# Attention operands of an eight-head kernel: the high half of v written by VectorE from the loaded v, and q and k copied by one ScalarE instruction

## The chip, the core and the metric

The kernel runs on one core of a Trainium2 chip. A core has five engines that run their own instruction queues in order and wait for each other by semaphores: PE (TensorE: matmuls and transposes into PSUM), DVE (VectorE), ACT (ScalarE), POOL (GpSimd) and SP, which here only issues transfers. Sixteen DMA engines move data between memory and the core, and also transpose blocks of 16-bit values. The metric is the time of one execution on the device in microseconds (us); lower is better.

## What is computed

An attention layer with a bias that a small network makes from positions, then two feed-forward blocks (a Fourier mixing block and a gated block), each on 4 batches of 576 positions. The change touches the attention alone:

```python
B, H, S, D = 4, 8, 576, 64
scores = (1 / np.sqrt(D)) * np.matmul(q, k.transpose(0, 1, 3, 2))
scores = scores + bias                      # one 576x576 bias per head, from w1, b1, w2
scores = scores - np.max(scores, axis=-1, keepdims=True)
attn = np.exp(scores)
attn = attn / (np.sum(attn, axis=-1, keepdims=True) + 1e-09)
attn_out = np.matmul(attn, v)
# ... attn_out then goes through two feed-forward blocks on 512 columns
```

## The kernel before

**Numbers in two halves.** Single-precision products are made from parts that TensorE multiplies fast. A value is split into a high half (the value rounded to a shorter form) and a low half (the value minus its high half), and a product is the sum of three matmuls: high by high, high by low, low by high. For q and k the short form is fp32r, for v and for the exponentials it is fp16. v is first multiplied by a power of two, `vs`, that `v_scale` finds from all of v.

**Stages.** The bias phase comes first (`bias_phase`, 48 blocks): POOL, ACT and PE make masks and products, and DVE evicts each block of bias into memory on the core (`evict`). Attention follows, in 72 steps `d` of two units each. A unit is one tile of 128 positions of one head. Sixteen pairs of heads (4 batches by 4 pairs) pass through the steps, two pairs in nine steps; step `c = d % 9` counts within these nine.

**One step of the loop** (the last loop of `attention_phase`; the program order of every engine is the order in which the Python code issues, since the schedule is manual):

- DVE subtracts for the transposed exponentials of the step before (`flip_low`, L477).
- ACT makes the two exponentials `P` of unit pair `d-1` (`soft`, L428).
- PE makes the 12 score matmuls of pair `d` (`scores`, L392), then five transposes `turn` of one unit (`flip`, L468), which ACT rounds to fp16 (`pt`, L470), and the products with v of pair `d-6` (`back`, L494, 28 to 60 small matmuls into `po`).
- For every second pair the transposition goes by DMA: ACT rounds the exponentials (`high`, L439), POOL subtracts the low half (`low`, L445, `hl`), and SP issues a DMA transpose (`turn` in the code, L458).
- DVE adds the bias to the scores and takes the maximum (`total`, L405, `s`), twice.
- At `c` of 3, 4 and 8 of the products (six steps later, so in steps 0, 1 and 5), DVE normalises `po` (`finish`: L514 `ri`, L518, L523 or L532).

The score tiles and the `turn` tile share three PSUM buffers, so that each `turn` waits until `flip_low` has read the one before.

**The preparation of a pair of heads** (`prep`, a generator that the loop advances twice a step, from `c` of 0 and of 5 on): q, k and v of the pair lie in `raw`, loaded by SP steps earlier (`load`). The first advance issues the rounding of k and q on ACT (L366, L367) and the second POOL's low half `kl` (L369). In the next step the third advance, between DVE's two `total`, issues POOL's `ql` (L371), and the fourth, after the second `total` and after `finish` has issued `ri`, issues POOL's scaling of v in place (L374). The fifth advance, a step later, issues ACT's high half of v (L376) and POOL's low half (L377). The first pair's preparation is spread over the bias phase, at blocks 8, 12, 16, 44 and 45.

`P` has four buffers, `hl` three, the halves of q and k two, `vp` (the two halves of v) three.

Of the kernel before, what the change touches and what calls it, by code (L numbers as in the profile page):

```python
# [9 lines left out]
F32 = mybir.dt.float32  # L10
F32R = mybir.dt.float32r
# [3 lines left out]
AF = mybir.ActivationFunctionType  # L15
ALU = mybir.AluOpType
PSUM = bass.MemoryType.PSUM

B, H, S, D = 4, 8, 576, 64
# [33 lines left out]
QW = S + 64  # L53
RAW = 2 * (S + 2 * QW)
# [8 lines left out]
def pool(tc, **kw):  # L63

    return tc.tile_pool(reuse_waits="tile", **kw)
# [263 lines left out]
def attention_phase(tc, nc, io, vs, bias, biasl, raw, xd, ident, after, es, right):  # L329
# [6 lines left out]
    tp = e1.enter_context(pool(tc, name="qk", bufs=2, side="right"))  # L336
    rq, st, live, pts, outs, xs, hls, mms, Ps = {}, {}, {}, {}, {}, {}, {}, {}, {}
# [12 lines left out]
    def load(n, nm):  # L350
        b, p = pairs[n]
        o, w = {"q": (0, QW), "k": (QW, S), "v": (QW + S, QW)}[nm]
        o += RAW // 2 * (n % 2)
        t = raw[:, o : o + w]
        if nm == "v":
            t = t.rearrange("p (t d) -> p t d", t=5)
        nc.sync.dma_start(out=t, in_=io[nm][b, p])
        rq.setdefault(n, {})[nm] = t

    def prep(n):  # L360

        r = rq.pop(n)
        T = {nm: tp.tile([128, S if nm[0] == "k" else QW], F32R, tag=nm, name=nm) for nm in ("kh", "kl", "qh", "ql")}
        T["v"] = vps[n % 3]
        st[n] = T
        nc.scalar.activation(out=T["kh"], in_=r["k"], func=AF.Copy)  # L366
        nc.scalar.activation(out=T["qh"], in_=r["q"], func=AF.Copy)  # L367
        yield
        nc.gpsimd.tensor_tensor(out=T["kl"], in0=r["k"], in1=T["kh"].bitcast(F32), op=ALU.subtract)  # L369
        yield  # L370
        nc.gpsimd.tensor_tensor(out=T["ql"], in0=r["q"], in1=T["qh"].bitcast(F32), op=ALU.subtract)  # L371
        yield
        vv = r["v"].rearrange("p t (h d) -> p t h d", h=2)
        nc.gpsimd.tensor_scalar(out=vv, in0=vv, scalar1=vs[:, 0:1], scalar2=None, op0=ALU.mult)  # L374
        yield
        nc.scalar.activation(out=T["v"][:, :, :, 0:64], in_=vv, func=AF.Copy)  # L376
        nc.gpsimd.tensor_tensor(out=T["v"][:, :, :, 65:129], in0=vv, in1=T["v"][:, :, :, 0:64], op=ALU.subtract)  # L377
        yield

    def scores(d):  # L380
# [155 lines left out]
    def store(d):  # L536
# [8 lines left out]
        for a in range(2):  # L545
            f = 128 * p + (64 * a if ahead(n) else 64 - 64 * a)
            nc.sync.dma_start(out=xd[b][512:S, f : f + 64], in_=x[64 * a : 64 * a + 64, 4, 0:64])

    yield [lambda n=n, nm=nm: load(n, nm) for n in range(2) for nm in "kqv"]
    yield from prep(0)  # L550
    yield True
    wp = es.enter_context(pool(tc, name="att", bufs=3))
# [12 lines left out]
    for d in range(nd + L5 + 2):  # L565
# [8 lines left out]
        n = 2 * (d // 9) + (c >= 5)  # L574
        if us and c in (0, 5) and n + 1 < len(pairs):
            nxt = prep(n + 1)
# [32 lines left out]
        if us and n + 2 < len(pairs):  # L609
            for nm in {0: "k", 1: "q", 2: "v"}.get(c - 5 * (c >= 5), ""):  # L610
                load(n + 2, nm)
# [1298 lines left out]
```

## Time and profile before

| | |
|---|---|
| time, median of 3 runs | 1056.87 us (1053.0 to 1058.15) |
| the profiled execution: its time, its span | 1050.65 us, 1048.9 us |
| mean granted TensorE clock of the profiled execution | 0.987 |
| busy over the span: PE, DVE, ACT, POOL | 94%, 63%, 51%, 29% |
| instructions: PE, DVE, ACT, POOL | 10571, 1736, 1000, 226 |

How to read it: the busy shares are averages over stages that differ. POOL works almost only in the bias phase and in attention, the first third of the span; after that PE is busy nearly without a pause in the feed-forward blocks. The profiled execution was 1.7 us longer than its span, which is what lies around the span.

### The profile page before, as it was taken

The page shows a single profiled execution, that of the slowest core. Times are in us where ns is not written, and L with a number is a line of the kernel's source. Part 1 is how long each engine was busy: PE and PEld are TensorE (multiplying, and loading weights), DVE is VectorE, ACT ScalarE, POOL GpSimd, SP SyncE. Part 2 cuts the span into 40 slices and gives each one's busy share as a digit, 9 for nine tenths or more (in the row PEclk, how much of TensorE's full clock was granted, in tenths as well). Part 3 has the DMA queues.
Part 4 walks back from the last instruction along what each step waited for, and adds up shares of the span by engine and source line. Part 5 has one row for each costly group of instructions (what it writes and reads, how often), then busy time and mean ns, then how long its engine had stood idle before and what let it go on. Part 6 is the DMA issues. An engine that isn't in the chain of part 4 may idle for free.

```text
span 1048.9 us, 25378 instructions
## 1 busy us (share of the span) xinstructions
PE 989.2 (94%) x10571; PEld 910.7 (87%) x10571; DVE 659.7 (63%) x1736; ACT 534.1 (51%) x1000; POOL 303.1 (29%) x226
## 2 busy tenths in 40 slices
PE   9898888988888899899999999999999999999998
PEld 6777787877778677899999999999999898989897
DVE  6888787888788887778944333244962556261611
ACT  6987888989898456444411112122542353334322
POOL 6998777788785000000000000000011111010100
PEclk9999799999999999999999999999999999999999
DMA  9882377889786601335300000001340000001001
GB/s 311 307 292 85 83 173 168 194 187 198 166 184 135 189 23 41 101 122 181 122 1 2 1 1 1 1 2 61 102 137 2 1 1 11 32 11 41 9 33 50
DMA packets 121339, 98.55 MB, mean 94 GB/s; under 512 B 86532, under 2 KB 97032, under 8 KB 121224
## 3 DMA queue, kind: packets, MB, share of 16 engines
q1 hardware_dynamic: 118488, 90.73, 32.3%
q10 hardware_dynamic: 2592, 5.31, 1.4%
q8 instruction: 82, 1.34, 0.5%
q0 software_dynamic: 144, 0.89, 0.2%
q14 instruction: 33, 0.27, 0.1%
HBM read 67.42 MB, written 9.44 MB: 73 GB/s over the span
## 4 chain that ended last, share of the span: by engine, by line
PE 71%; DVE 9%; POOL 7%; ACT 4%; issue 4%; DMA 3%; SPq 1%; ACTq 0%; POOLq 0%; DVEq 0%
PE h L1336 18%; PE acc L1372 18%; PE psp L1508 5%; PE pu L1483 4%; PE po L1530 4%; PE pv L1431 4%; POOL hl L445 3%; PE y L854 3%; PE sc L392 2%; PE bps L272 2%; PE po L494 2%; PE pre L253 2%; DVE pt L477 2%; PE turn L468 2%; PE D L884 2%
## 5 line engine op out<-in xcount | busy, mean ns | idle before, releaser
L1340 ACT ACTIVATE gh<-h 128x256 fp32r<-128x256 f32 x144 | 55.2, 383 | 245.8 <-PE h L1336 240.2
L1341 DVE SCALAR_TENSOR_TENSOR gl<-h,gh 128x256 fp32r<-128x256 f32 x144 | 60.9, 423 | 170.6 <-ACT gh L1340 170.0
L1336 PE MATMUL h<-uh,wh 128*128 128x256 f32 x576 | 161.5, 281 | 2.2 <-DVE gl L1341 2.0
L1372 PE MATMUL acc<-gh,wh 128*128 128x256 f32 x576 | 163.0, 283 | 0.0
L1372 PE MATMUL acc<-gh,wl 128*128 128x256 f32 x576 | 161.0, 280 | 1.4 <-DVE wl L1044 1.4
L1336 PE MATMUL h<-uh,wl 128*128 128x256 f32 x576 | 160.9, 279 | 1.1 <-DVE wl L1044 1.1
L1372 PE MATMUL acc<-gl,wh 128*128 128x256 f32 x576 | 160.8, 279 | 0.0
L1336 PE MATMUL h<-ul,wh 128*128 128x256 f32 x576 | 160.7, 279 | 0.0
L1128 POOL MEMSET w<- 64x288 f32 x2 | 0.7, 335 | 434.5 <-DVE wsq L1025 434.4
L1336 PEld LDWEIGHTS h<-uh,wh 128*128 128x128 f32 x576 | 109.0, 189 | 2.9 <-DVE gl L1341 2.4
L1372 PEld LDWEIGHTS acc<-gh,wl 128*128 128x128 f32 x576 | 108.4, 188 | 1.7 <-DVE wl L1044 1.7
L1336 PEld LDWEIGHTS h<-uh,wl 128*128 128x128 f32 x576 | 108.4, 188 | 1.3 <-DVE wl L1044 1.3
L1372 PEld LDWEIGHTS acc<-gh,wh 128*128 128x128 f32 x576 | 108.9, 189 | 0.4
L1372 PEld LDWEIGHTS acc<-gl,wh 128*128 128x128 f32 x576 | 108.9, 189 | 0.3
L1336 PEld LDWEIGHTS h<-ul,wh 128*128 128x128 f32 x576 | 108.8, 189 | 0.0
L428 ACT ACTIVATE P<-s,mm 128x576 f32<-128x576 f32 x144 | 103.4, 766 | 5.5 <-DVE mm L420 5.3
L445 POOL TENSOR_TENSOR hl<-P,hl 128x1024 f16<-128x1024 f32 x68 | 86.1, 1288 | 19.6 <-ACT hl L439 11.8
L468 PE MATMUL turn<-ident,P 128*128 128x128 f32 x380 | 58.3, 285 | 29.8 <-DVE pt L477 29.4
L494 PE MATMUL po<-vp,pt 128*128 128x65 f16 (+3 forms) x2324 | 83.5, 195 | 2.2 <-DMA pt<-hl 0.8
L494 PEld LDWEIGHTS <-pt 128*128 128x128 f16 (+1 forms) x2324 | 80.1, 101 | 5.6 <-issue 2.0
L243 POOL TENSOR_SCALAR mask<-tx,w,nb 128x576 f16<-128x576 f32 x36 | 81.9, 2286 | 9.8 <-DVE xt L218 6.1
L468 PEld LDWEIGHTS turn<-ident,P 128*128 128x128 f32 x380 | 41.3, 142 | 42.2 <-DVE pt L477 16.1
(252 smaller groups left out, 2507.1 us busy)
## 6 DMA issues: line engine op xcount, KB each, us to landing
w<-in_w_ch SPq DMA_DIRECT2D x32, 512.0 KB, 3.6
tx<-in_c_xm SPq DMA_DIRECT2D x36, 288.0 KB, 5.8
vld<-in_v ACTq DMA_DIRECT2D x16, 320.0 KB, 4.6
raw<-in_q SPq DMA_DIRECT2D x16, 320.0 KB, 4.1
raw<-in_v SPq DMA_DIRECT2D x16, 320.0 KB, 4.4
raw<-in_k SPq DMA_DIRECT2D x16, 288.0 KB, 3.4
xd<-x SPq DMA_DIRECT2D x16, 256.0 KB, 4.1
w<-in_w_in SPq DMA_DIRECT2D x8, 512.0 KB, 3.5
```

The source lines that it names most:

```text
L243: nc.gpsimd.tensor_scalar(out=m, in0=rows.pop(n), scalar1=w1p, scalar2=nb, op0=ALU.mult, op1=ALU.is_gt)
L428: nc.scalar.activation(out=P[:, x, 0:S], in_=s, func=AF.Exp, bias=mm[:, 1, x : x + 1], scale=1.0)
L445: nc.gpsimd.tensor_tensor(out=hl[:, :, o : o + c], in0=P[:, :, j : j + c], in1=hl[:, :, j : j + c], op=ALU.subtract)
L468: nc.tensor.transpose(t[:, 128 * k : 128 * k + 128], P[:, 128 * k : 128 * k + 128], ident)
L494: nc.tensor.matmul(out=po[c, t % 4, 0:w], lhsT=pt[:, x, c], rhs=vp[:, j, hh, f : f + w], start=(i == 0), stop=(i == len(seq) - 1),)
L1336: nc.tensor.matmul(out=h, lhsT=st[:, q], rhs=mv[:, k], start=(n == 0), stop=(n == 11))
L1340: nc.scalar.activation(out=gh, in_=h, func=AF.Relu)
L1341: nc.vector.scalar_tensor_tensor(out=gl, in0=h, scalar=0.0, in1=gh.bitcast(F32), op0=ALU.max, op1=ALU.subtract)
L1372: nc.tensor.matmul(out=acc[x, d // 2][:, d % 2], lhsT=st[:, q], rhs=mv, start=(e == 0 and d % 2 == 0 and n == 0), stop=(e == NF - 1 and d ...
L1431: nc.tensor.matmul(out=p, lhsT=st[:, k, c], rhs=W[1, k][part], start=(n == 0), stop=(n == 11))
L1483: nc.tensor.matmul(out=p[:, 0:CH], lhsT=st[:, q], rhs=mv[:, kk, e], start=(n == 0), stop=(n == 11))
L1508: nc.tensor.matmul(out=p[:, 0:CH], lhsT=st, rhs=mv, start=(n == 0), stop=(n == len(seq) - 1))
```

## The change

`prep` alone changes, with a helper entry in `load`. q and k of a pair lie next to each other in `raw`, and the halves of both now lie in one tile each, `qkh` and `qkl`. One ACT instruction over 1216 columns makes `qkh` in place of two over 576 and 640. The high half of v is no longer made by ACT from the v that POOL has scaled; DVE makes it from the loaded v, multiplying by `vs` and rounding to fp16 in one instruction, issued just ahead of POOL's scaling. POOL's scaling overwrites the loaded v, so it now waits for DVE; POOL's low half of v waits for DVE where it waited for ACT.

```diff
-        rq.setdefault(n, {})[nm] = t
+        o = RAW // 2 * (n % 2)
+        rq.setdefault(n, {"qk": raw[:, o : o + QW + S]})[nm] = t
 
     def prep(n):
 
         r = rq.pop(n)
-        T = {nm: tp.tile([128, S if nm[0] == "k" else QW], F32R, tag=nm, name=nm) for nm in ("kh", "kl", "qh", "ql")}
+        hi, lo = (tp.tile([128, QW + S], F32R, tag=x, name=x) for x in ("qkh", "qkl"))
+        T = {"qh": hi[:, 0:QW], "kh": hi[:, QW:], "ql": lo[:, 0:QW], "kl": lo[:, QW:]}
         T["v"] = vps[n % 3]
         st[n] = T
-        nc.scalar.activation(out=T["kh"], in_=r["k"], func=AF.Copy)
-        nc.scalar.activation(out=T["qh"], in_=r["q"], func=AF.Copy)
+        nc.scalar.activation(out=hi, in_=r["qk"], func=AF.Copy)
         yield
-        nc.gpsimd.tensor_tensor(out=T["kl"], in0=r["k"], in1=T["kh"].bitcast(F32), op=ALU.subtract)
-        yield
-        nc.gpsimd.tensor_tensor(out=T["ql"], in0=r["q"], in1=T["qh"].bitcast(F32), op=ALU.subtract)
-        yield
+        for nm in "kq":
+            h = T[nm + "h"].bitcast(F32)
+            nc.gpsimd.tensor_tensor(out=T[nm + "l"], in0=r[nm], in1=h, op=ALU.subtract)
+            yield
         vv = r["v"].rearrange("p t (h d) -> p t h d", h=2)
+        vh = T["v"][:, :, :, 0:64]
+        nc.vector.tensor_scalar(out=vh, in0=vv, scalar1=vs[:, 0:1], scalar2=None, op0=ALU.mult)
         nc.gpsimd.tensor_scalar(out=vv, in0=vv, scalar1=vs[:, 0:1], scalar2=None, op0=ALU.mult)
         yield
-        nc.scalar.activation(out=T["v"][:, :, :, 0:64], in_=vv, func=AF.Copy)
-        nc.gpsimd.tensor_tensor(out=T["v"][:, :, :, 65:129], in0=vv, in1=T["v"][:, :, :, 0:64], op=ALU.subtract)
+        nc.gpsimd.tensor_tensor(out=T["v"][:, :, :, 65:129], in0=vv, in1=vh, op=ALU.subtract)
         yield
```

Two places show what moves. The first is ACT's order in attention, from the `high` of one step through the preparation of a pair that starts at `c` of 5 (`kh`, `qh` and `vp_87` belong to it), before:

```order
L439 ACTIVATE hl<-P_3089 128x2x576
L366 ACTIVATE kh<-raw 128x576
L367 ACTIVATE qh<-raw 128x640
L428 ACTIVATE P_3091<-s,mm 128x576 x2
L470 ACTIVATE pt<-turn 128x640
L428 ACTIVATE P_3092<-s,mm 128x576 x2
L470 ACTIVATE pt<-turn 128x640
L439 ACTIVATE hl<-P_3091 128x2x576
L376 ACTIVATE vp_87<-raw 128x10x64
L428 ACTIVATE P_3089<-s,mm 128x576 x2
```

The same stretch of ACT's order with the change (buffers are numbered anew, and lines below the edit have moved by two):

```order
L441 ACTIVATE hl<-P_3086 128x2x576
L368 ACTIVATE qkh<-raw 128x1216
L430 ACTIVATE P_3088<-s,mm 128x576 x2
L472 ACTIVATE pt<-turn 128x640
L430 ACTIVATE P_3089<-s,mm 128x576 x2
L472 ACTIVATE pt<-turn 128x640
L441 ACTIVATE hl<-P_3088 128x2x576
L430 ACTIVATE P_3086<-s,mm 128x576 x2
```

The copy into `vp_87` no longer stands between `high` and the next two exponentials, and two copies are one.

The second place is DVE's order in the step `c` of 1, where `finish` normalises the short tiles of two pairs (`ri`, `x`) and a preparation is at its fourth advance, before:

```order
L405 ISA s,mm<-sc,lowa 128x576
L405 ISA mm 128x1
L420 TENSOR_SCALAR mm<-mm 128x1
L514 TENSOR_SCALAR ri<-po,vs 128x2
L518 RECIPROCAL ri<-ri 128x2
L532 TENSOR_SCALAR x<-po,ri 128x64 x2
L477 TENSOR_TENSOR pt<-turn,pt 128x640
```

And the same stretch of DVE's order with the change:

```order
L407 ISA s,mm<-sc,lowa 128x576
L407 ISA mm 128x1
L422 TENSOR_SCALAR mm<-mm 128x1
L516 TENSOR_SCALAR ri<-po,vs 128x2
L376 TENSOR_SCALAR vp_86<-raw,vs 128x10x64
L520 RECIPROCAL ri<-ri 128x2
L534 TENSOR_SCALAR x<-po,ri 128x64 x2
L479 TENSOR_TENSOR pt<-turn,pt 128x640
```

The new instruction stands behind `ri` and ahead of the reciprocal, `x` and the subtraction into `pt`. In the step `c` of 6 it stands between the second `total` and the subtraction into `pt`. POOL's order does not move.

## Rows read from the trace of the kernel before

**Rows 1.** Busy time of each engine, 60 us of attention (18 steps).

```profile
148.70:208.90 60.20, 52.23 (x892) 47.28 (x889) 50.31 (x147) 52.81 (x77) 48.09 (x37) 0.97 0.79 173
```

**Rows 2.** Waits of ACT, then POOL, 103.3 to 332 us: total us, times, longest.

```profile
ACT vp L376 <- POOL raw L374: 4.1, 3, 1.4
...
POOL kl L369 <- ACT kh L366: 18.2, 6, 3.7
...
POOL vp L377 <- ACT vp L376: 11.6, 11, 3.5
```

**Rows 3.** Timeline near 157 us: start, us, what, idle before and releaser.

```profile
153.49 1.02 PE L494 MATMUL po<-vp,pt 128*128 128x65 f16 x28
...
154.29 1.16 ACT L439 ACTIVATE hl<-P 128x1152 f16<-128x1152 f32 x1
...
156.81 0.75 ACT L376 ACTIVATE vp<-raw 128x640 f16<-128x640 f32 x1 [1.37 <-POOL raw L374]
...
159.50 0.82 DVE L477 TENSOR_TENSOR pt<-turn,pt 128x640 f16<-128x640 f32 x1 [2.13 <-ACT pt L470]
...
160.38 1.12 PE L468 MATMUL turn<-ident,P 128*128 128x128 f32 x5 [2.09 <-DVE pt L477]
...
161.30 1.73 PE L494 MATMUL po<-vp,pt 128*128 128x65 f16 x28
```

**Rows 4.** Timeline of a step with c of 1, near 196 us.

```profile
194.00 1.56 POOL L371 TENSOR_TENSOR ql<-raw,qh 128x640 fp32r<-128x640 f32 x1
...
196.37 0.22 DVE L514 TENSOR_SCALAR ri<-po,vs 128x2 f32<-128x2 f32 x1 [0.81 <-PE po L494]
...
198.19 0.74 PE L468 MATMUL turn<-ident,P 128*128 128x128 f32 x5 [0.87 <-DVE pt L477]
```

**Rows 5.** Windows of 1 us: busy PE, PEld, DVE, ACT, POOL, granted clock, DMA.

```profile
161.00:162.00 1.00, 1.00 (x16) 0.94 (x15) 0.93 (x4) 0.46 (x1) 0.48 (x2) 0.50 0.42 157
...
221.00:222.00 1.00, 1.00 (x31) 0.99 (x29) 0.96 (x5) 0.68 (x2) 0.63 (x2) 1.00 0.60 217
```

**Rows 6.** Timeline after another step with c of 1, near 172 us.

```profile
171.88 0.74 ACT L376 ACTIVATE vp<-raw 128x640 f16<-128x640 f32 x1
...
174.56 0.82 DVE L477 TENSOR_TENSOR pt<-turn,pt 128x640 f16<-128x640 f32 x1 [0.67 <-ACT pt L470]
```

**Rows 7.** Two lines of DVE: count, min/median/max ns, first and last start, shape.

```profile
L1019 DVE TENSOR_SCALAR wsq<-wsq x44: 414/418/429, 362.7 to 773.2; 128x512 int32<-128x512 int32 x44
...
L228 DVE TENSOR_SCALAR xt<-xt,gs x8: 431/439/1065, 8.3 to 63.0; 128x360 f32<-128x360 f32 x8
```

**Rows 8.** Timeline of two scalings on DVE, and of POOL's mask beside each.

```profile
34.07 1.06 DVE L228 TENSOR_SCALAR xt<-xt,gs 128x360 f32<-128x360 f32 x1
...
34.08 2.29 POOL L243 TENSOR_SCALAR mask<-tx,w,nb 128x576 f16<-128x576 f32 x1
...
48.36 2.28 POOL L243 TENSOR_SCALAR mask<-tx,w,nb 128x576 f16<-128x576 f32 x1
...
49.02 0.43 DVE L228 TENSOR_SCALAR xt<-xt,gs 128x360 f32<-128x360 f32 x1
```

**Rows 9.** Timeline of DVE in another step with c of 6, with POOL beside it.

```profile
150.87 2.54 POOL L445 TENSOR_TENSOR hl<-P,hl 128x1024 f16<-128x1024 f32 x2
...
152.00 0.82 DVE L477 TENSOR_TENSOR pt<-turn,pt 128x640 f16<-128x640 f32 x1 [0.24 <-ACT pt L470]
```

**Rows 10.** Timeline of a step with c of 6, near 184 us.

```profile
183.40 0.82 DVE L477 TENSOR_TENSOR pt<-turn,pt 128x640 f16<-128x640 f32 x1
...
184.75 0.76 PE L468 MATMUL turn<-ident,P 128*128 128x128 f32 x5
```

**Rows 11.** Timeline of the end of the bias phase.

```profile
98.65 0.75 ACT L376 ACTIVATE vp<-raw 128x640 f16<-128x640 f32 x1 [1.75 <-POOL raw L374]
...
103.31 0.58 PE L392 MATMUL sc<-kh,qh 64*128 64x288 f32 x1 [1.55 <-DVE lowb L308]
```

**Rows 12.** DMA transposes: count and median us from issue to landing.

```profile
pt<-hl SPq DMA_TRANSPOSE x34, 4.8
```

## The prediction

> **What bounds the kernel now.** I read the span in slices first: the change lies in the end of the bias phase and in attention, and nothing after. In attention the windows come next. Over 18 steps, 60.2 us, PE is busy 52.2, ACT 52.8, DVE 50.3 and POOL 48.1 us [rows 1]: no engine is full, all are near 80 to 88%, so the stage is paced by engines that wait for each other in order, and only a wait that the others inherit is worth anything. A step takes 60.2 / 18 = 3.3 us.
>
> The waits show which of them the change touches [rows 2]. ACT's high half of v waits for POOL's scaling three times, 4.1 us in all; POOL's low half waits for ACT 11 times, 11.6 us; POOL's `kl` waits for `kh` six times, 18.2 us. The last two are idle time of POOL. The first is different, since behind `vp` on ACT stand the next exponentials and the copy `pt`.
>
> The timeline at one of the three shows the inheritance [rows 3]. ACT's `hl` ends at 154.29 + 1.16 = 155.45; `vp` starts only at 156.81, when POOL is done, and ends at 157.56. The exponentials and `pt` follow, so DVE's subtraction L477 has idled 2.13 us, and PE's `turn`, which needs the PSUM buffer that L477 frees, 2.09 us. And the clock falls: `turn` then takes 1.12 us where it elsewhere takes 0.74 [rows 4], and 28 products 1.73 where shortly before they took 1.02. The granted clock there is 0.50, TensorE's 1.2 GHz; at the second of the three places it stays 1.00, 2.4 GHz, after the same idle time [rows 5].
>
> The pattern returns every 18 steps, and a period holds four preparations. I call them A (start near 149, the stall above; 3 in all), B (near 163; 3), C (near 180; 4, with the one near 120) and D (near 192; 4). With pair 1 at the start of attention that is 15, and pair 0 lies in the bias phase.
>
> **The change, part by part.**
>
> *ACT loses `vp`.* At A the exponentials need not wait for POOL: they may start at 155.4 instead of 157.5. L477 could then follow DVE's own work at once. I count 2.0 us per place, three times: −6.0. The clock that fell cost (1.12 − 0.74) + (1.73 − 1.02) = 1.1 us; I count it twice, −2.2, since the third place reads like the first. At B `vp` takes 0.74 us of ACT, some 0.6 from start to start, and DVE's L477 then waits 0.67 us for ACT [rows 6]: up to 0.6 comes back. At C and D ACT has room and nothing comes back.
>
> *DVE gains the high half of v,* 640 columns. The trace before has no such instruction. Nearest: a scaling of 512 columns on the core takes 0.42 us, one of 360 columns with a scalar read per partition 0.43 undisturbed [rows 7]; a 640-column subtraction that reads PSUM takes 0.82 [rows 3]. So 0.42 to 0.82; I take 0.55, near the scalings, as both its operands are on the core too.
>
> Something can hold it up. The 360-column scaling took 1.06 us at its slowest. That one started as a mask of POOL began (34.07 against 34.08), while one that began 0.66 us into a mask, at 49.02, took 0.43 [rows 8]. So POOL can hold a DVE scaling up by 1.06 − 0.43 = 0.63 us, but not for its whole length: the mask at 48.36 ran on to 50.64. The Trainium skill (SBUF — State Buffer, Who interferes with whom) says that these two engines share a port pair, and that whoever issues first has it "for the whole instruction; the other fully blocks"; by that rule the 49.02 scaling would have lasted past 50.64, and the rows here don't agree. I price the hold-up at 0 in the sum and at 0.63 in the range.
>
> Where the 0.55 falls:
>
> - A: between `total` and L477, which idled 0.24 us there [rows 9]: 0.3 each, +0.9.
> - B: behind `ri`, +0.55 against the 0.6 that ACT gives back: 0.
> - C: L477 ended at 183.40 + 0.82 = 184.22 and PE's `turn` started at 184.75, PE being busy until then [rows 10]: 0.5 of cover, so 0. Without it 0.55 each, +2.2.
> - D: behind `ri`, which has waited for PE, and ahead of `x` and L477, for which PE already idles 0.87 us [rows 4]: nothing covers it, +0.55 four times, +2.2.
> - Pair 0: the start of attention on PE waits for DVE's last evictions (1.55 us before 103.31), while ACT's 1.75 us of waiting at 98.65 has no one behind it [rows 11]: +0.55.
> - Pair 1: DVE is idle there between scores: 0.
>
> *POOL's scaling now waits for DVE.* Queued behind it are POOL's `vp` and the `hl` pieces. At A the DVE slot (151.7) lies ahead of POOL's scaling. At D it doesn't: POOL's `ql` ended at 195.56, while `vh` would end at 196.37 + 0.22 + 0.55 = 197.1, so POOL is 1.6 us late there. The cover: `low` is issued three steps ahead of the products that need it, 3 × 3.3 = 10 us, of which `hl` takes 2.54 [rows 9] and the transpose 4.8 [rows 12]; some 2.6 us stay. I cost it at 0; with the cover gone it is up to 1.6 × 4 = 6.4 us. In return POOL no longer waits for ACT (11.6 us), which no one else waited for.
>
> *q and k in one instruction.* One start-up less, perhaps 0.1 to 0.2 us of ACT fifteen times; `kl` starts up to one q copy later. POOL idles 3 us ahead of `kl` where it waits, so I cost both at 0; the bounds are −1.5 us (every 0.1 felt) and, on POOL, part of the cover above.
>
> **The sum**, against the profiled execution: −6.0 − 2.2 + 0.9 + 2.2 + 0.55 = −4.55 us, 1050.65 → 1046.1 us. That execution lies 6.2 us below the median of the runs shown; the difference carried to the median gives 1056.87 − 4.55 = 1052.3 us, 0.43% faster. About 0.5%, 5.3 us, is what a measurement of this kernel can tell from no change, so my forecast is a small gain at the edge of it.
>
> **Rivals.**
>
> *More gain.* `vh` costs 0.42 (−0.13 at A, D and pair 0, eight places: −1.0), B keeps its ACT gain (−0.5 three times), the clock counts at all three A (−1.1) and some of the merged copy is felt (−0.5): −4.55 − 4.1 = −8.7, 1048.2. For it: ACT is the busiest engine [rows 1]. Against: at D and C ACT isn't waited for.
>
> *Held up by POOL: slower.* DVE waits for the rest of POOL's instruction at A, B and pair 0, seven places (at C and D POOL itself waits for DVE then). At A `vh` would start at 151.7 with `hl` running to 153.41: 1.7 us, seven times +11.9, so +7.3 and 1064.2. It decides from (5.3 + 4.55) / 7 = 1.4 us per place on. For it: the slowest scaling; against: that one lost only 0.63, and others nothing [rows 7, 8]. The rule of the Trainium skill quoted above describes this mechanism.
>
> *The stall is taken over.* At A another wait ends where `vp` ended, for instance the exponentials wait for a `P` buffer that POOL's `hl` still reads, or the late `hl` at D reaches PE. Then the −8.2 goes: +3.65, 1060.5. For it: POOL has been the late engine at A. Against: POOL saves its own waits for ACT.
>
> *The clock falls elsewhere.* At D and B PE's idle time of 0.87 us becomes 1.4. Idle time of 2.09 us brought the clock down in some places, 0.87 in none that I read; 1.4 is not shown. Seven times 1.1 us would be +7.7: 1060.0.
>
> **How the numbers follow.** Forecast 0.37, more gain 0.27, held up 0.14, taken over 0.12, clock 0.10. The forecast's own range is 1049.5 to 1055: it takes in 0.42 for `vh`, and 0.63 of hold-up at some of the seven places. Its part below 1051.6 (over 0.5% faster) is some 0.4 of 0.37, so faster is 0.27 + 0.15 = 0.42. Slower than 1062.2 are most of held up and a little of the next two: 0.15. Same: 0.43. With 0.82 for `vh` (+0.27 at eight places and at B and C, +4.1 in all) and 0.63 of hold-up at seven (+4.4) the sum is +3.9, 1060.8. The range of 8 in 10 is 1047 to 1061: below it a tail of more gain, above it held up.
>
> **What would show it.** Right: no idle time of 2 us on DVE L477 and PE `turn` near 157, 217 and 277, no half clock behind it; the period of 18 steps falls from 60.2 to some 58.7 us; PE's idle time ahead of `turn` at D grows from 0.87 to 1.4; the DVE row for the high half reads about 0.55 us. Wrong: that row has a median over 1.2 us (held up); a wait of DVE L477 for ACT at A as long as before, with ACT now waiting for something else (taken over); half clock in windows behind D (clock); PE's wait for the transposes over 1 us (POOL late).

## The result, and the profile after

The changed kernel took 1060.87 us (median of 20 runs, 1055.83 to 1064.80), the kernel before in the same sessions 1055.05 us (median of 20 runs): a ratio of 1.0052, 95% interval 1.0037 to 1.0068. So the change makes the kernel 0.5% slower, by 4 to 7 us. The prediction was 1052.3 us. The profiled execution of the changed kernel took 1059.89 us, its span is 1057.6 us.

Line numbers behind the edit are 2 higher than before (L477, DVE's subtraction, is L479 now, PE's `turn` L470). The new DVE instruction, all 16 of them (count, min/median/max ns, first and last start, shape):

```profile
L376 DVE TENSOR_SCALAR vp<-raw,vs x16: 548/1006/2223, 98.3 to 323.5; 128x640 f16<-128x640 f32 x16
```

The 0.55 us of the sum, a pick between 0.42 and 0.82, is its minimum; that it fits to the digit is luck. But its median is 1.01 and its maximum 2.22. Place A, near 157, which answers to [rows 3]:

```profile
155.40 1.43 POOL L372 TENSOR_TENSOR qkl<-raw,qkh 128x576 fp32r<-128x576 f32 x1 [4.23 <-ACT qkh L368]
...
156.77 2.78 POOL L447 TENSOR_TENSOR hl<-P,hl 128x1024 f16<-128x1024 f32 x2
...
157.05 2.22 DVE L376 TENSOR_SCALAR vp<-raw,vs 128x640 f16<-128x640 f32 x1
...
159.19 0.81 DVE L479 TENSOR_TENSOR pt<-turn,pt 128x640 f16<-128x640 f32 x1
...
160.06 0.77 PE L470 MATMUL turn<-ident,P 128*128 128x128 f32 x5 [1.87 <-DVE pt L479]
...
160.87 0.70 ACT L472 ACTIVATE pt<-turn 128x640 f16<-128x640 f32 x1 [2.29 <-PE turn L470]
```

ACT's stall behind POOL's scaling is gone, as forecast. But DVE's high half of v, issued 0.28 us into POOL's `hl`, ends only at 159.27. A 0.55 us instruction that ends there began at 158.72, near the end of the first of the two `hl` pieces (it took 2.15 us from 156.77). In this profile all ten that were issued while POOL ran a subtraction ended 0.35 to 0.36 us after the end of one. The second piece in turn is late: the pair took 2.78 us where it took 2.54 before [rows 9]. L479 stands behind, and PE waits 1.87 us for it, as against 2.09 before. A wait of DVE for POOL has taken the place of ACT's wait for POOL. At B, where POOL runs `hl`, and at D, where POOL waits for DVE:

```profile
171.69 0.22 DVE L516 TENSOR_SCALAR ri<-po,vs 128x2 f32<-128x2 f32 x1 [0.93 <-PE po L496]
171.82 1.26 DVE L376 TENSOR_SCALAR vp<-raw,vs 128x640 f16<-128x640 f32 x1
...
174.54 0.74 PE L470 MATMUL turn<-ident,P 128*128 128x128 f32 x5 [1.90 <-DVE pt L479]
...
201.48 0.22 DVE L516 TENSOR_SCALAR ri<-po,vs 128x2 f32<-128x2 f32 x1 [0.81 <-PE po L496]
201.62 0.55 DVE L376 TENSOR_SCALAR vp<-raw,vs 128x640 f16<-128x640 f32 x1
...
203.63 0.74 PE L470 MATMUL turn<-ident,P 128*128 128x128 f32 x5 [1.19 <-DVE pt L479]
```

The `turn` behind B in the kernel before:

```profile
169.45 0.74 PE L468 MATMUL turn<-ident,P 128*128 128x128 f32 x5 [0.87 <-DVE pt L477]
```

So PE's wait at B, which the sum had at no change, grew from 0.87 to 1.90 us (1.91 and 1.88 at the other two), and at D from 0.87 to 1.19.

At C DVE's high half takes 1.0 us, and 1.96 at the first C near 125, where the sum had a price of 0. There PE's wait is followed by a lower clock, as at A before [rows 3, 5]:

```profile
124.14 2.93 POOL L372 TENSOR_TENSOR qkl<-raw,qkh 128x576 fp32r<-128x576 f32 x2 [0.50 <-ACT qkh L368]
...
125.46 1.96 DVE L376 TENSOR_SCALAR vp<-raw,vs 128x640 f16<-128x640 f32 x1
...
128.21 1.20 PE L470 MATMUL turn<-ident,P 128*128 128x128 f32 x5 [1.73 <-DVE pt L479]
129.20 1.84 PE L496 MATMUL po<-vp,pt 128*128 128x65 f16 x30
```

`turn` takes 1.20 us there in place of 0.77, and the windows give the granted clock:

```profile
126.00:128.00 2.00, 0.48 (x8) 0.25 (x4) 2.00 (x2) 2.00 (x3) 1.55 (x2) 1.00 1.17 205
128.00:130.00 2.00, 1.79 (x20) 1.73 (x21) 1.81 (x7) 0.92 (x2) 2.00 (x2) 0.60 0.78 281
```

The 18 steps from step 15 on take 60.6 us and the next 18 59.8, where before they took 60.1 and 59.4: the period did not fall. In a window of 60.2 us, as long as that of [rows 1], what has changed is who is busy (PE, PEld, DVE, ACT, POOL, granted clock, DMA):

```profile
155.00:215.20 60.20, 50.28 (x886) 45.59 (x886) 54.22 (x151) 49.78 (x68) 48.66 (x37) 1.00 0.83 173
```

ACT is 3.0 us lighter, DVE 3.9 heavier. The waits from 100 to 365 us show POOL's `kl`, which answers to [rows 2]: 18.2 us in six waits became

```profile
POOL qkl L372 <- ACT qkh L368: 23.4, 14, 4.2
...
POOL raw L377 <- DVE vp L376: 4.6, 5, 2.8
```

For the experiments I use two numbers of each profile, read from the starts of DVE's first `total` (L405 before, L407 now) of a step: when step 0 starts, which tells how long the bias phase took, and the 60 steps from step 3 to step 63, which is attention without its ends. Before: 105.13 and 309.82 − 112.64 = 197.2. After: 108.25 and 317.15 − 115.77 = 201.4. So the bias phase ended 3.1 us later and attention lost 4.2 us. Of the 4.2 us, 2.2 lie in steps 3 to 15, which hold the first C and the first D, 1.8 around the other C and D, and 0.2 around A and B (steps 15 to 24, 33 to 42, 51 to 60), where the sum had its gain. These two profiles lie 9.2 us apart, the two medians 5.8 us.

### The profile page after: what moved, and what is told of

Same layout as the page of the kernel before. It is cut to its first block, busy times and chain, and to the rows that moved or that the text cites. A ratio compares the mean times of both kernels' runs of the same rounds, so it can differ in the third digit from the quotient of the medians.

```text
span 1057.6 us, 25386 instructions
## 1 busy us (share of the span) xinstructions
PE 987.7 (93%) x10571; PEld 909.4 (86%) x10571; DVE 676.1 (64%) x1752; ACT 522.7 (49%) x968; POOL 305.3 (29%) x226
## 4 chain that ended last, share of the span: by engine, by line
PE 73%; DVE 14%; issue 4%; DMA 3%; ACT 3%; POOL 2%; SPq 0%; ACTq 0%; DVEq 0%; POOLq 0%
PE h L1338 19%; PE acc L1374 18%; PE psp L1510 5%; PE pu L1485 4%; PE po L1532 4%; PE po L496 4%; PE sc L394 3%; PE pv L1433 3%; PE y L856 3%; PE turn L470 2%; DVE pt L479 2%; DVE s L407 2%; PE bps L272 2%; PE D L886 2%; PE pre L253 1%
## 5 line engine op out<-in xcount | busy, mean ns | idle before, releaser
L1338 PEld LDWEIGHTS h<-ul,wh 128*128 128x128 f32 x576 | 108.9, 189 | 0.0
L470 PE MATMUL turn<-ident,P 128*128 128x128 f32 x380 | 57.6, 283 | 36.3 <-DVE pt L479 36.3
L470 PEld LDWEIGHTS turn<-ident,P 128*128 128x128 f32 x380 | 41.1, 142 | 48.2 <-issue 31.3
```

Of the source, the lines that this page charges most:

```text
L470: nc.tensor.transpose(t[:, 128 * k : 128 * k + 128], P[:, 128 * k : 128 * k + 128], ident)
L1338: nc.tensor.matmul(out=h, lhsT=st[:, q], rhs=mv[:, k], start=(n == 0), stop=(n == 11))
```

## The experiments

Ratios are to the kernel before, run beside each on the same chip, with 95% intervals. The table has the two numbers of every profile and the time that DVE's high half of v took in its 15 places of attention (15 × 0.55 = 8.25 us if undisturbed).

| kernel | ratio | step 0 starts | steps 3 to 63 | high half on DVE |
|---|---|---|---|---|
| before; again | 1 | 105.1; 107.8 | 197.2; 196.7 | – |
| changed; again | 1.0052 | 108.3; 110.9 | 201.4; 203.2 | 17.8; 17.1 |
| one copy of q, k alone | 1.0020 | 109.5 | 202.6 | – |
| v edit alone | 0.9968 | 105.4 | 194.0 | 12.6 |
| changed, accumulator form | 0.9949 | 107.5 | 193.2 | 13.2 |
| changed, pair 0 split | 1.0061 | 109.6 | 203.4 | 17.7 |
| v edit, q copied first | 1.0060 | 110.0 | 202.9 | 17.0 |
| v edit, accumulator form | 0.9961 | 103.7 | 193.5 | 13.2 |
| high half on ACT from loaded v | 0.9947 | 104.8 | 190.5 | – |
| changed, pair 0 later | 1.0031 | 107.5 | 203.2 | 17.6 |
| v edit, one copy at pair 0 | 0.9983 | 108.1 | 193.9 | 12.6 |
| changed, `hl` from one tensor | one run | 109.4 | 200.0 | 12.4 |

**One half of the change at a time.** First the one copy, with v as before:

```diff
...
-        nc.scalar.activation(out=T["kh"], in_=r["k"], func=AF.Copy)
-        nc.scalar.activation(out=T["qh"], in_=r["q"], func=AF.Copy)
+        nc.scalar.activation(out=hi, in_=r["qk"], func=AF.Copy)
```

> Only q and k in one ACT instruction; v as in the kernel before. Theory hold-up (POOL's instruction in progress keeps DVE's high half of v waiting): it plays no part here, the ratio to the kernel before is 0.999 to 1.001, and ACT's stall ahead of `vp` at A is back with 1.4 us. Rival merged copy (ACT waits in the bias phase for q's load too, 1.9 us in the changed kernel, and POOL's kl starts later): the first attention score is 2 us later than before and the ratio is 1.002 or above; if the whole loss is here, 1.005.

Measured: 1.0020 (0.9996 to 1.0044). The interval holds both no change and +4.6 us; the one profile is 5.4 us slower in attention. It shows where: ACT's `vp` waits for POOL longer and once more than before [rows 2]:

```profile
ACT vp L377 <- POOL raw L375: 7.8, 4, 2.0
```

PE's waits for DVE's subtraction add up to no more than before (24.7 us in the 60 steps, 25.1 before), but PE was busy 176.1 us in place of 170.4, at a granted clock of 0.93 in place of 0.97.

Then the v edit, with q and k as before:

```diff
...
+        nc.vector.tensor_scalar(out=vh, in0=vv, scalar1=vs[:, 0:1], scalar2=None, op0=ALU.mult)
...
-        nc.scalar.activation(out=T["v"][:, :, :, 0:64], in_=vv, func=AF.Copy)
...
```

> Only the high half of v made by DVE; q and k in two ACT instructions as before. Hold-up: the DVE instruction takes 1.9 to 2.2 us at A and about 1.3 at B, 0.55 where POOL idles, and the ratio to the kernel before is 1.003 to 1.006. Rival merged copy: without it ACT's saved stall shows, 0.996 to 1.000. Rival plain cost (0.55 us on DVE, no hold-up needed): 1.003 too, but with 0.55 at every place.

Measured: 0.9968 (0.9945 to 0.9990), faster, and against what I expected of the hold-up: it is there, but shorter. Place A of this kernel:

```profile
150.68 1.41 POOL L369 TENSOR_TENSOR kl<-raw,kh 128x576 fp32r<-128x576 f32 x1 [3.69 <-ACT kh L366]
...
152.05 2.78 POOL L446 TENSOR_TENSOR hl<-P,hl 128x1024 f16<-128x1024 f32 x2
152.87 1.68 DVE L375 TENSOR_SCALAR vp<-raw,vs 128x640 f16<-128x640 f32 x1
154.46 0.81 DVE L478 TENSOR_TENSOR pt<-turn,pt 128x640 f16<-128x640 f32 x1
...
155.33 0.77 PE L469 MATMUL turn<-ident,P 128*128 128x128 f32 x5 [1.32 <-DVE pt L478]
```

DVE issues 0.82 us into `hl` here, 0.28 in the changed kernel, so 0.54 less is left to wait for. POOL waited 3.69 us for the copy of k, and 4.23 there: 0.54 again. That gave a second theory: the one copy makes `kl` late by 0.54 us, everything on POOL behind it is as late, and whoever waits for POOL pays.

**The hold-up taken away.** The form that also sums into an accumulator, with nobody reading the sum, in the changed kernel:

```diff
+    vas = [vp.tile([128, 1], F32, name=f"va{x}") for x in range(3)]
...
-        nc.vector.tensor_scalar(out=vh, in0=vv, scalar1=vs[:, 0:1], scalar2=None, op0=ALU.mult)
+        va = vas[n % 3]
+        nc.vector.tensor_scalar(
+            out=vh, in0=vv, scalar1=vs[:, 0:1], scalar2=None, op0=ALU.mult, op1=ALU.add, accum_out=va
+        )
```

> The changed kernel with DVE's high half of v in the form that also writes an accumulator (a column that nothing reads). Hold-up, and the form escapes it: one length at all 16 places, an estimate of 0.85 us from 0.82 of the 640-column subtraction; A then gains 1.2 us three times, B 0.4 three times, D loses 0.3 four times, and the stall of 2 us behind 125 with its half clock goes: 4 to 6 us below the changed kernel, ratio to the kernel before 0.999 to 1.001. If this form is held up as well, the lengths at A stay at 2 us or more and the ratio at 1.005. Rival plain cost: 0.3 us more at 16 places, ratio 1.008 to 1.010.

Measured: 0.9949 (0.9928 to 0.9971), 5.4 us faster than before and, by the two ratios, about 11 us faster than the changed kernel; I had expected 4 to 6. All 16 take one length, and A beside `hl` is undisturbed on both engines:

```profile
L378 DVE TENSOR_SCALAR_CACHE_REDUCE vp<-raw,vs x16: 872/874/884, 97.7 to 314.6; 128x640 f16<-128x640 f32 x16
```

```profile
153.84 2.54 POOL L451 TENSOR_TENSOR hl<-P,hl 128x1024 f16<-128x1024 f32 x2
...
154.14 0.88 DVE L378 TENSOR_SCALAR_CACHE_REDUCE vp<-raw,vs 128x640 f16<-128x640 f32 x1
...
155.81 0.77 PE L474 MATMUL turn<-ident,P 128*128 128x128 f32 x5 [0.55 <-DVE pt L483]
```

An instruction that alone is 0.33 us longer, with a read of the accumulator of 0.08 us behind it, makes the kernel 1% faster, because DVE doesn't wait for POOL. This falsifies the rival that DVE's plain time is the cost. The Trainium skill (SBUF — State Buffer, Who interferes with whom) names the scaling as an operation that can take the ports shared with GpSimd, and excepts the form that writes out its accumulator; these rows agree.

The same form with two copies tests whether the one copy costs or saves by itself; against the kernel above:

```diff
...
-        nc.scalar.activation(out=hi, in_=r["qk"], func=AF.Copy)
+        nc.scalar.activation(out=T["kh"], in_=r["k"], func=AF.Copy)
+        nc.scalar.activation(out=T["qh"], in_=r["q"], func=AF.Copy)
```

> The v edit with the accumulator form, q and k in two ACT instructions as before. Hold-up theory: 0.88 us at every place; against the v edit alone 2.6 us less at four places of hold-up and up to 2 us more where it took 0.55, so about as the v edit alone, 0.995 to 0.997. If the merged copy saves ACT time of its own, the changed kernel with the accumulator form (0.9949) stays ahead; if it only costs, this one is ahead, 0.992 to 0.994.

Measured: 0.9961 (0.9933 to 0.9989); 193.5 us for the 60 steps, 193.2 with one copy. Where nobody waits for POOL, the late `kl` costs nothing, and the saved start-up brings nothing.

**Late `kl` without the one copy.** The v edit alone with its two copies in the other order:

```diff
+        nc.scalar.activation(out=T["qh"], in_=r["q"], func=AF.Copy)
         nc.scalar.activation(out=T["kh"], in_=r["k"], func=AF.Copy)
-        nc.scalar.activation(out=T["qh"], in_=r["q"], func=AF.Copy)
```

> The high half of v by DVE (held-up form), q and k in two ACT instructions, but q copied first: kh is then as late as in the merged copy, and in the bias phase ACT waits for q's load as there. Theory now (the merged copy delays kl on POOL by some 0.55 us, POOL's next instructions come that much later, and DVE's high half of v waits for them that much longer): lengths as in the changed kernel, 1.9 to 2.2 us at A, 1.25 at B, 1.0 at C, ratio to the kernel before 1.002 to 1.006. Rival (it is the single instruction or its tiles, not the order): lengths as with the v edit alone, 1.3 to 1.7, 0.71 and 0.56, ratio 0.996 to 0.999.

Measured: 1.0060 (1.0034 to 1.0086). The swap of two lines on ACT, with the same work, turns −0.3% into +0.6%. The lengths of the high half are the changed kernel's or a little more (the first C, issued at 127.74, just ahead of the end of `kl` near 127.9, took 0.56):

```profile
L375 DVE TENSOR_SCALAR vp<-raw,vs x16: 548/1092/2320, 99.5 to 326.8; 128x640 f16<-128x640 f32 x16
```

So the order does it: the single instruction is not needed. Pair 0 has the other order too, so a part of the 0.9% can lie in the bias phase (step 0 at 110.0); the 60 steps alone are 9.0 us longer than with the v edit. PE's waits for DVE's subtraction make up 5.1 us of that (31.4 against 26.3), and PE's busy time 4.2 (170.7 against 166.5, at a granted clock of 0.97 against 0.99).

**ACT makes the high half from the loaded v.** No DVE instruction, no wait for POOL:

```diff
+        vh = T["v"][:, :, :, 0:64]
+        nc.scalar.activation(out=vh, in_=vv, func=AF.Copy, scale=vs[:, 0:1])
         nc.gpsimd.tensor_scalar(out=vv, in0=vv, scalar1=vs[:, 0:1], scalar2=None, op0=ALU.mult)
         yield
-        nc.scalar.activation(out=T["v"][:, :, :, 0:64], in_=vv, func=AF.Copy)
...
```

> The kernel before, but ACT makes the high half of v straight from the loaded v, scaling it itself, one prep step sooner, so it waits for no engine; DVE has no part. If what the change is worth is ACT's stall at A (three times 1.4 to 2 us and the clock behind it): 5 to 8 us saved, ratio 0.992 to 0.995. Rival (ACT has no room one step sooner, its 0.74 us are felt at B, C and D): 0.997 to 1.000.

Measured: 0.9947 (0.9923 to 0.9972), with the accumulator form the fastest here. The 18 steps from step 15 on take 57.5 us in place of 60.1, though ACT is as busy in the 60 steps as before (173.9 us); the 16 ACT instructions that make the high half took 0.83 us each. A window of 58.5 us:

```profile
150.00:208.50 58.50, 50.83 (x889) 46.12 (x890) 51.17 (x148) 53.70 (x77) 48.89 (x38) 1.00 0.90 182
```

The stall was worth the gain, not ACT's busy time.

**The bias phase.** In the changed kernel ACT's copy for pair 0 waits for q's load; PE then waits 3.19 us for ACT's mask, and the clock falls (windows of 4 us, after; before, this window has a granted clock of 1.00):

```profile
31.06 1.22 ACT L368 ACTIVATE qkh<-raw 128x1216 fp32r<-128x1216 f32 x1 [1.89 <-DMA raw<-in_q]
```

```profile
32.00:36.00 4.00, 3.13 (x42) 2.57 (x42) 0.14 (x1) 3.34 (x7) 2.40 (x3) 0.60 1.04 394
```

Three runs asked whether that wait is the 3 us. Pair 0 alone with two copies:

```diff
-        nc.scalar.activation(out=hi, in_=r["qk"], func=AF.Copy)
+        if n == 0:
+            nc.scalar.activation(out=T["kh"], in_=r["k"], func=AF.Copy)
+            nc.scalar.activation(out=T["qh"], in_=r["q"], func=AF.Copy)
+        else:
+            nc.scalar.activation(out=hi, in_=r["qk"], func=AF.Copy)
```

> The changed kernel, but pair 0 (in the bias phase) copies k and q in two ACT instructions, k first, as before; the other 15 pairs keep the one copy. Merged copy waits for q's load: ACT's wait of 1.9 us near 31 goes, the first attention score comes about 2 us sooner than in the changed kernel, ratio to the kernel before 1.003. Hold-up alone: nothing moves, 1.005.

Measured: 1.0061 (1.0040 to 1.0081), no better. ACT still waited 0.59 us for q and 0.73 for another load just ahead, and step 0 started at 109.6. Pair 0 two blocks later:

```diff
-Q_PREP = 8, 12, 16, 44, 45
+Q_PREP = 10, 14, 18, 44, 45
```

> The changed kernel, pair 0's copies two bias blocks later (blocks 10, 14, 18 for 8, 12, 16), so that q has landed when ACT comes to the copy. If the 3 us that the bias phase loses in the profile are ACT's wait for q's load: no wait for the load on ACT near 36, first attention score near 105.5, ratio to the kernel before 1.002 to 1.003. If they are chance or come from elsewhere: first score near 108 and 1.005.

Measured: 1.0031 (1.0010 to 1.0052), which fits both. The wait for q is gone, but ACT's reads of `vld` waited 1.26 and 1.72 us for loads, and step 0 started at 107.5. The reverse, one copy at pair 0 alone, against the changed kernel:

```diff
-        nc.scalar.activation(out=hi, in_=r["qk"], func=AF.Copy)
+        if n == 0:
+            nc.scalar.activation(out=hi, in_=r["qk"], func=AF.Copy)
+        else:
+            nc.scalar.activation(out=T["kh"], in_=r["k"], func=AF.Copy)
+            nc.scalar.activation(out=T["qh"], in_=r["q"], func=AF.Copy)
```

> The reverse of the run that split pair 0: pair 0 in the bias phase has the one copy of q and k, the other 15 pairs two copies, k first; high half of v by DVE. If the 3 us of the bias phase are pair 0's one copy waiting for q's load: first attention score near 108, ratio to the kernel before 0.999 to 1.001. If they come by chance or from elsewhere: first score near 105.4 and the ratio of the v edit alone, 0.996 to 0.998. In both cases the lengths of the high half of v are those of the v edit alone (1.3 to 1.7 at A, 0.71 at B, 0.56 at C), since kl is early again.

Measured: 0.9983 (0.9965 to 1.0001), step 0 at 108.1; attention as with the v edit alone, 193.9 us, with the same lengths (12.6 us). Its ratio lies 1.6 us above the v edit's, with intervals of about ±2 us. And both kernels once more, unchanged:

> The kernel before, profiled once more, for the bias phase: if its end is late by chance of the loads, the first attention score here lies anywhere from 104 to 110; if only kernels with a late kl or one copy are late, it is at 105.1 within 0.7 as in the first profile.

> The changed kernel, profiled once more: by chance, first attention score anywhere from 104 to 110; if the change makes it late, 107.5 to 110 as in the first profile (108.25). The lengths of the high half of v repeat: 1.8 to 2.2 at A, 1.25 at B, 1.0 at C, 0.55 at D.

Measured: the kernel before at 107.8, the changed one at 110.9. So chance moves step 0 by 2.7 us in either. The six profiles with k copied first at pair 0 have a mean of 106.1 (103.7 to 109.6), the eight others 108.9 (107.5 to 110.9): a difference of 2.8 us that fits the wait, with ranges that overlap. But the length of the wait for q doesn't follow step 0: in the second profile of the changed kernel, the latest of all, it was 0.27 us (ACT had waited 2.53 us for a load just ahead), and with the accumulator form 0.46 us. The attention numbers repeat far better, 0.5 and 1.8 us.

**What on POOL holds DVE up.** `hl` from one tensor in place of two, in the changed kernel (the low half of the even steps' probabilities is zero):

```diff
-                nc.gpsimd.tensor_tensor(
-                    out=hl[:, :, o : o + c], in0=P[:, :, j : j + c], in1=hl[:, :, j : j + c], op=ALU.subtract
+                nc.gpsimd.tensor_scalar(
+                    out=hl[:, :, o : o + c], in0=P[:, :, j : j + c], scalar1=0.0, scalar2=None, op0=ALU.mult
```

> The changed kernel with POOL's `hl` pieces as a product of P alone with zero, one tensor read in place of two: the low half of the even steps' probabilities is left out (zeros). If POOL holds DVE's high half of v for the whole of its instruction only when it reads two tensors, as beside the mask at pair 0 (0.94 us, with the mask running on for 1.1 us more): at A and B, where `hl` runs beside it, 0.55 to 0.95 us in place of 2.2 and 1.25, while at C, where the unchanged qkl runs beside it, it stays at 1.0 or more. If any POOL instruction holds it: 2 us or more at A and B.

Measured at A, B and the second A:

```profile
158.40 3.27 POOL L447 TENSOR_SCALAR hl<-P 128x1024 f16<-128x1024 f32 x2
158.67 1.12 DVE L376 TENSOR_SCALAR vp<-raw,vs 128x640 f16<-128x640 f32 x1
...
171.09 3.52 POOL L447 TENSOR_SCALAR hl<-P 128x1024 f16<-128x1024 f32 x2
172.95 1.29 DVE L376 TENSOR_SCALAR vp<-raw,vs 128x640 f16<-128x640 f32 x1
...
218.15 3.26 POOL L447 TENSOR_SCALAR hl<-P 128x1024 f16<-128x1024 f32 x2
219.35 0.56 DVE L376 TENSOR_SCALAR vp<-raw,vs 128x640 f16<-128x640 f32 x1
```

Only in part as expected. At A it took 1.12, 0.56 and 1.12 us and at B 1.29, 0.55 and 0.55; three of the six lie in the expected 0.55 to 0.95. The 1.12 is half of the changed kernel's 2.22 and ends 1.4 us before POOL's piece does. The 1.29 is no shorter than the changed kernel's 1.26, and it ended 0.35 us after the end of POOL's first piece, as beside two tensors; why that one was held isn't shown. At three of the four C, where `qkl` is unchanged, it took 1.0. So five of six were not held to the end. The edit also turns a subtraction into a scaling that is longer, so that the number of tensors read is the cause is argued, not shown. The one run took 1062.6 us. Its 60 steps are 1.4 to 3.2 us shorter than the changed kernel's, not 8 as with the accumulator form: POOL takes 3.27 us for what took 2.54, and PE's waits for DMA transposes are 3.3 us in them, where the changed kernel's were 0.3 and 0.7.

## Why the prediction was wrong

- *ACT loses `vp`, −6.0 and the clock −2.2*: right in mechanism and in size, where nothing else comes in between. The kernel that takes only this away, with the high half on ACT from the loaded v, takes 8.6 us less around A and B (85.5 against 94.1); it loses 2 us in the other steps and gains 6.4 us in the 60. In the changed kernel PE still waits 1.5 to 1.9 us at A, since DVE's wait has come in.
- *DVE gains 0.55*: right in length where nothing holds it up. At D PE's wait grew from 0.87 [rows 4] to 1.19, by 0.32 and not by 0.55.
- *"I price the hold-up at 0 in the sum and at 0.63 in the range"*: the step that failed first. DVE's instruction lasted as long as the rest of POOL's, and 0.35 us more. Over 15 places it was 17.78 − 8.25 = 9.5 us of DVE: 1.3 to 1.7 at A, 0.7 at B, and 0.45 at C (1.4 at the first), where I had said that POOL waits for DVE; it ran `qkl`. At B PE then waited 1.90 us, where I had set the 0.55 off against ACT's gain. The rows behind the price were scalings beside POOL's mask [rows 8], which reads one tensor. What runs beside it in attention reads two, and held DVE to its end in every case with over 0.2 us left. I carried a rate from one kind of POOL instruction to another.
- *The rule dismissed.* The Trainium skill's sentence that the other engine "fully blocks" (SBUF — State Buffer, Who interferes with whom) is what the rows of attention show beside two-tensor instructions of POOL. Beside one-tensor ones the rows mostly don't agree: at pair 0 the instruction took 0.94 us from 98.33 while the mask ran from 98.10 for 2.28. One of six in the run with `hl` from one tensor does agree (the 1.29).
- *The one copy, "`kl` starts up to one q copy later. POOL idles 3 us ahead of `kl` where it waits, so I cost both at 0"*: wrong in its logic. POOL idles because it waits for that very copy, so the 3 us are no cover: the 0.54 us pass to everything behind. With the hold-up this is what decides: v edit alone −3 us in the 60 steps, with a late `kl` +4 to +6. Where no engine waits for POOL it costs nothing (193.2 against 193.5); where ACT does, with v as before, the one profile lost 5.4 us. So the interaction was missing from the sum. The start-up saved is 0.1 us (`qkh` takes 1.21 where `kh` and `qh` took 1.31 from start to end).
- *POOL late at D, 0*: right. POOL's scaling waits 1.2 us for DVE there, and PE's waits for transposes are 0.8 us in all of attention, as before.
- *Rival held up*: its mechanism is the one found, at 1.7 us at A as it said; it left out C and took too much at B. It had 0.14. Its sign, a median over 1.2 us, did not show (1.01), because five of the 16 places had POOL idle and C and pair 0 were held up for less. The measured 1060.9 us lies just inside the range of 8 in 10, and that is luck: up there the range counted on 0.82 us for `vh` and 0.63 of hold-up.
- *Rival the clock falls elsewhere*: PE's idle time at B became 1.9 us, not 1.4. `turn` behind it still took 0.74 at the first B; behind the third the granted clock was 0.50 from 296 to 298 us. It fell behind the first C too (0.60). So this had a share in the loss, behind waits that the hold-up had lengthened.
- *Pair 0, +0.55*: 0.94 measured. Whether the bias phase loses 2.8 us more to the wait for q's load stays open: the profiles lean that way, the lengths of the wait don't follow them, and the ratios of the kernels that split and merged pair 0 don't settle it.

## What to carry to other kernels

Idle time ahead of an instruction covers a delay only if the delayed thing is not what that instruction waits for. When an instruction moves to DVE beside a busy POOL, look up what POOL runs at that moment and price the rest of that instruction, not a rate from another kind of it; a form of the operation that is longer by itself can be the faster one. Two edits of which one gains and the other isn't shown to cost anything by itself (0.9968, and 1.0020 with an interval that holds 1) can meet in a queue between them, so time each alone.

## What the hardware showed that I had not expected

- A 0.55 us scaling on DVE took up to 2.32 us beside a POOL subtraction of two tensors, and POOL's pair of pieces took 2.78 in place of 2.54 then: each waits for the other's instruction to end. The same scaling with an accumulator took 0.87 to 0.88 everywhere.
- Issued 0.09 to 0.10 us before the end of one POOL subtraction, with another queued behind it, the scaling was held by the second one too, in four profiles (1.96 and 1.97 us at the first C); issued 0.10 us before such an end in the run with `hl` from one tensor, and 0.18 before with q copied first, it went through in 0.56. What decides isn't shown.
- Beside a one-tensor POOL instruction it was held up when issued 0.2 to 0.3 us after that one's start (0.94 and 1.12), not at 1.2 us (0.55), and again at 1.86 us (1.29), to 0.35 us after that one's end. Why isn't shown.
- The bias phase of one and the same kernel ended 2.7 us apart in two profiles. In the later one of the kernel before ACT waited 0.6 and 0.5 us for loads near 28 to 30 us, and the granted clock from 32 to 36 us was 0.57 in place of 1.00.
